# Where the spread reciprocals are copied: two exp steps behind their product, on VectorE in one unit, in an attention + MoE kernel

## The chip, the core and the metric

The kernel runs on one core of a Trainium2 chip. A core has TensorE (PE, the matmul array), VectorE (DVE), ScalarE (ACT), GpSimd (POOL) and SyncE (SP, here a queue for transfers). Each engine works through its own instructions in order and waits for the others by semaphores. The metric is the device time of one launch in microseconds; before the change the median of three runs is 494.64 us (494.27 to 496.47).

## The reference

```python
def _attn_ref(q, k, v):                 # (8, 12, 448, 64) each, f32
    scores = (1 / sqrt(64)) * q @ k.transpose(0, 1, 3, 2)
    m = max(scores, axis=-1, keepdims=True)
    e = exp(scores - m)
    attn = e / (sum(e, axis=-1, keepdims=True) + exp(-m) + 1e-09)
    return attn @ v

def _moe_ref(x, w_in, w_out):           # x (3584, 768), w_in (768, 2048), w_out (2048, 768)
    h = x @ w_in
    g = h * tanh(log1p(exp(h)))         # mish
    return g @ w_out

out = _moe_ref(attention, its heads side by side, w_in, w_out)
```

Eight batches of 12 heads of attention, with one added to the softmax's denominator, feed one MLP with a mish in the middle.

## The kernel before, in words

The work is cut in pairs of heads (6 pairs for a batch, 48 in all) and units of three pairs. The order of all instructions is written out by hand; no scheduler moves any. An "exp step" is one fourth of a pair: a step `s` of 0 to 3, numbered `idx = 4 * pair + s`. At a step, ACT computes the exps of one or two score tiles (`exps`, two instructions at steps 0 to 2, one at step 3). Then PE computes the scores of the step three further on, into one of three PSUM tiles `sc0` to `sc2`, and DVE finds their maxima (`negm`, in `scores`).

Everything else is put between the steps:

- `load_pair` (SP's queue), `cast_pair` (POOL): q, k and v come in and are cast to bf16.
- `transpose_pair` (PE), `evac_qk` (DVE or ACT): q and k are turned, and copied out of PSUM.
- `denominators` (DVE, POOL): the reciprocals `rden` of the row sums, and `hl`, the same as a sum of two bf16 numbers.
- `normalise`: `eT`, the turned exps, by a transposing DMA on SP's queue. For pairs 0 to 4 one of four quarters, and for pairs 5 to 7 (the dict `BY_PE`) all four, are turned by PE (`turn_on_pe`) and copied from PSUM by DVE, or by ACT where `TURN_BY_ACT` says so.
- `spread_rden` (pairs 0 to 11): 16 small matmuls spread a pair's reciprocals over the rows of a PSUM bank, from where ACT copies them to `rb` in SBUF.
- `av_pair`: eight matmuls multiply `eT` with v. For pairs 0 to 11, DVE multiplies the result by `rb` into `xT`; from pair 12 on (`LATE_DIV`) the exps were divided earlier, and DVE only copies.

There are two spare PSUM banks, `mo0` and `mo1`. `mo_take()` hands out one; it is given back where its copy out of PSUM is issued. Such copies are not issued at once: they go to the list `late`, which `flush_late()` issues behind the exps of the next step.

The stages: the head (pairs 0 to 5, the loop over `HEAD`), unit 2 (pairs 6 to 8), unit 3 (pairs 9 to 11), then units 4 to 15. Behind the steps of units 2 and later stand eight groups of matmuls with `w_in` and the mish on ACT (`mm1_mish`) for an earlier batch. From unit 4 on, matmuls with `w_out` (`mm2_part`) fill the gaps between the steps. The dicts `AV_AT` and `RDEN_AT` say at which step `n` of the unit a product or a spread stands in units 2 to 4: the outer key is the unit less 2, the inner one `n`, the value the pair.

In the head before the change, step 0 of pair p has `transpose_pair(p + 2)`, `denominators(p - 1)` and the turned quarter of p - 1; step 1 has the spread of p - 3, step 3 the product of p - 3.

Of the kernel before, what the change touches and what calls it, by code (L numbers as in the profile page):

```python
# [19 lines left out]
def kernel(  # L20
# [9 lines left out]
    nc = tc.nc  # L30

    B, H, S, D = q.shape
# [3 lines left out]
    NT = 4  # L36
# [63 lines left out]

    loaded, casted, qkT, att, xT, o_sbs, stats = {}, {}, {}, {}, {}, {}, {}
    av_with, av_read, rb = {}, {}, {}
    late = deque()

    def flush_late():
        while late:
# [2 lines left out]
    def mo_take():  # L109

        if not mo_free:
            flush_late()
        return mo_free.popleft()


    def load_pair(p):
# [205 lines left out]
            for i in range(n):  # L322
                att[p + i]["hl"] = hl[:, :, i, :]

    def spread_rden(p):

        own = mo_take()
        r = own[:, :]
        hl = att[p]["hl"]
        half = SP_ * NT - 3 * 128  # L330
        for at in range(4):
            for x in range(2):
                for h in range(2):
                    if at < 3:
                        rows, c, q0 = slice(0, 128), at + 4 * h, 128 * at + half * h
                    else:
                        rows, c, q0 = slice(half * h, half * h + half), 3, 3 * 128 * (1 - h)
                    n = rows.stop - rows.start
                    nc.tensor.matmul(  # L339
                        r[h * D : (h + 1) * D, q0 : q0 + n],  # L340
                        lhsT=hl[rows, x, c : c + 1].to_broadcast([n, D]),
                        rhs=ident[rows, rows],
                        start=(x == 0), stop=(x == 1),
                    )

        def evac():
            rb[p] = rb_pool.tile([128, S], FP32, tag="rb", name="rb")
            nc.scalar.copy(rb[p], r[:, 0:S])  # L348
            mo_free.append(own)

        late.append(evac)

    def normalise(p, dma=True):
        st = att[p]
# [30 lines left out]

        late.append(evac)

    def av_pair(p, bank=None, beside=None):
        b, hp = p // HP, p % HP
        eT = att[p]["eT"]  # L390
        v_bf = casted[p][2]
        if b not in xT:
            xT[b] = xT_pool.tile([128, DM_T, S], BF16, tag="xT", name="xT")
        av = mo_take() if bank is None else bank
        for j in range(NT):
            for h in range(2):
                if p >= DIAG_FROM:
                    by_h = eT[0:SP_, j, :].rearrange("c (i h r) -> c h i r", h=2, r=64)
                    e_h = by_h[:, h]
                else:  # L400
                    e_h = eT[0:SP_, j, h * S : (h + 1) * S]
                nc.tensor.matmul(  # L402
                    av[h * 64 : (h + 1) * 64, 0:S],
                    lhsT=v_bf[:, h, j * D : (j + 1) * D],
                    rhs=e_h,
                    start=(j == 0), stop=(j == NT - 1),
                )

        def evac():
            to = xT[b][:, hp, :]  # L410
            if p >= LATE_DIV:
                read = nc.vector.tensor_copy(out=to, in_=av[:, 0:S])  # L412
            else:
                read = nc.vector.tensor_tensor(
                    out=to, in0=av[:, 0:S], in1=rb.pop(p), op=ALU.mult
                )
            if beside is not None:
                av_read[beside] = read
            if bank is None:
                mo_free.append(av)  # L420

        late.append(evac)
        del att[p], casted[p], qkT[p]


# [94 lines left out]
    HEAD = HP  # L520

    BY_PE = {HEAD - 1: 1, HEAD: 0, HEAD + 1: STEPS}
    AV_AT = {0: {5: 3, 7: 4, 10: 5}, 1: {8: 6, 10: 7, 11: 8}}
    RDEN_AT = {0: {4: 3, 6: 4, 9: 5}, 1: {7: 6, 9: 7, 10: 8}, 2: {3: 10, 7: 11}}
    TURN_BY_ACT = {(HEAD - 1, 3), (HEAD, 3), (HEAD + 1, 2)}

    W_AT = ({1: 1, 5: 1, 9: 1}, {1: 1, 5: 1, 7: 1, 9: 1, 11: 1}, {1: 1, 3: 1, 5: 1, 7: 1})
    for p in range(UNIT_PAIRS):
# [13 lines left out]
    for p in range(HEAD):  # L542
        for s in range(STEPS):
            exps(p * STEPS + s)
            if s == 0 and p == 0:
                evac_qk(1, act=True)
            flush_late()
            if s == 2 and p < HEAD:
                evac_qk(p + 2, act=p % 2 == 0)
            scores_ahead(HEAD * STEPS + 3)  # L550
            if s == 0:
                transpose_pair(p + 2)
                if p:
                    denominators(p - 1)
                    turn_on_pe(p - 1, NT - 1)
            if s in (1, 3) and p == HEAD - 1:
                load_w(1)
            if s == 1 and p >= 3:
                spread_rden(p - 3)
            if s == 2:  # L560
                cast_pair(p + 3)
            if s == 3:
                if p >= 3:
                    av_pair(p - 3)
                if p + 5 < 10:
                    load_pair(p + 5)
                normalise(p, dma=p not in BY_PE)
    denominators(HEAD - 1)

    for u in range(UNITS_PER_B, N_UNITS + 2 * UNITS_PER_B):  # L570
        attn = u < N_UNITS
        filler = deque()
        for part in plan.get(u, []):
            filler.extend(mm2_part(*part))
        total, done, acc = sum(w for _, w in filler), 0, 0.0
        p0 = u * UNIT_PAIRS
        if attn and u >= first_mm2:
            av_with.update({p0 + i: p0 + i - UNIT_PAIRS for i in range(UNIT_PAIRS)})
        end = min((u + 1) * UNIT_PAIRS, N_PAIRS) * STEPS

        for n in range(steps):
            pi, s = divmod(n, STEPS)
            p, idx = p0 + pi, p0 * STEPS + n
            late_tp = u == UNITS_PER_B and n == STEPS
            if late_tp:
                transpose_pair(p0 + 2)
            exps(idx)
            if late_tp:
                evac_qk(p0 + 2)
            if u == UNITS_PER_B + 1 and n == 0:  # L590
                for j in range(2):
                    turn_on_pe(HEAD, j)
            flush_late()
            acc += weight[n]
            want = int(total * acc / sum(weight) + 1e-6)
            while done < want:
                fn, w = filler.popleft()
                fn()
                done += w
            scores_ahead(end)  # L600
            if n in LOAD_AT:
                load_pair(p0 + LOAD_AT.index(n) + LEAD)
                cast_pair(p0 + LOAD_AT.index(n) + LEAD - 1)
            spread = RDEN_AT.get(u - UNITS_PER_B, {})
            if n in spread:
                spread_rden(spread[n])
            early = AV_AT.get(u - UNITS_PER_B)
            if early is not None:
                if n in early:
                    av_pair(early[n])  # L610
                for pe, n0 in BY_PE.items():
                    first = 2 if pe == HEAD else 0
                    if pe // UNIT_PAIRS == u - 1 and n0 + first <= n < n0 + NT:
                        turn_on_pe(pe, n - n0, act=(pe, n - n0) in TURN_BY_ACT)
            elif s == (2 if pi else 0) and N_PAIRS <= p < N_PAIRS + UNIT_PAIRS:
                av_pair(p - UNIT_PAIRS)
            if u - UNITS_PER_B < len(W_AT):
                load_w(W_AT[u - UNITS_PER_B].get(n, 0))
        assert done == total

        moe = u < N_UNITS + UNITS_PER_B
        b, w = (u - UNITS_PER_B) // UNITS_PER_B, u % UNITS_PER_B
        nxt = p0 + UNIT_PAIRS
        todo = sorted(range(p0, nxt), key=lambda p: p in BY_PE)
        for f in range(FF_U):
            if moe:
                mm1_mish(b, w * FF_U + f)
            if u == UNITS_PER_B and f in (2, 6) or u == UNITS_PER_B + 1 and f == 1:
                load_w(1)
            if not attn:  # L630
                continue
            if f == 0:
                denominators(p0, UNIT_PAIRS)
                for p in todo if p0 < LATE_DIV else todo[:1]:
                    normalise(p, dma=p not in BY_PE)
            if f == 5 and u == UNITS_PER_B + 1:
                spread_rden(p0)
            if f == 4:
                scores_ahead(min(nxt * STEPS + 1, N_PAIRS * STEPS))
            if f in (1, 3, 5):  # L640
                transpose_pair(nxt + f // 2, bank=f // 2 % 2)
                evac_qk(nxt + f // 2)
            if f >= FF_U - 2:
                scores_ahead(min(nxt * STEPS + f - FF_U + 4, N_PAIRS * STEPS))
            if f in (3, FF_U - 1) and p0 >= LATE_DIV:
                p = todo[1 + f // (FF_U - 1)]
                normalise(p, dma=p not in BY_PE)
# [32 lines left out]
```

## Time and profile before

| | |
|---|---|
| median of three runs | 494.64 us |
| profiled execution, its own time | 492.1 us |
| its span, first to last instruction | 490.3 us |
| PE busy | 455.9 us (93%) |
| DVE busy | 356.3 us (73%) |
| ACT busy | 348.4 us (71%) |
| POOL busy | 103.3 us (21%) |
| mean granted clock of PE | 0.979 |

In the profile a row of the timeline has the start and the duration in us, the engine, the line of the kernel, the operation, out<-in, how many instructions were merged, and in brackets the idle time before them with who ended it. L296 are the exps, L283 the maxima, L339 the spread, L348 the copy `rb`, L376 a turned quarter and L380 its copy to `eT`, L402 the product with v, L414 its multiplication into `xT`, L431 and L437 the matmuls with `w_in` and the mish, L465 the copy of a finished output tile.

### The profile page before, as it was taken

To read this page: it belongs to the slowest core of one execution; us is meant where nothing else is said; L and a number is where in the kernel's file an instruction comes from. 1 tells how busy PE (TensorE), PEld (TensorE's weight loads), DVE (VectorE), ACT (ScalarE), POOL (GpSimd) and SP (SyncE) were. 2 spreads that over 40 slices of the span, in tenths; PEclk is the share of its full clock that TensorE was granted. 3 is DMA by queue.
4 is the path that set the end of the run, shared out by engine and by line. 5 is a ranking of instruction groups with operands and counts; after the bars stand their busy time and mean duration, and the time that the engine had idled before them with its cause. 6 is when DMAs were issued, how large, how long until landed. Compare 5 with 4: busy or idle time off the path is not lost.

```text
span 490.3 us, 9225 instructions
## 1 busy us (share of the span) xinstructions
PE 455.9 (93%) x3219; PEld 260.1 (53%) x3219; DVE 356.3 (73%) x706; ACT 348.4 (71%) x912; POOL 103.3 (21%) x184
## 2 busy tenths in 40 slices
PE   4676896898999999999999999999999999999996
PEld 2343553554555565555655555556555565556563
DVE  4887837657789898989989888889899988520011
ACT  5978778868788887978687978888797868402300
POOL 4533261423204040302213130404040200000000
PEclk9996698999999999999999999999999999999999
DMA  8999999999998969999899989997989786770122
GB/s 235 232 225 198 171 162 192 215 183 248 195 200 247 200 199 196 255 169 258 182 223 184 231 196 191 231 188 220 204 251 168 203 151 140 139 152 24 41 57 74
DMA packets 204975, 91.08 MB, mean 186 GB/s; under 512 B 161792, under 2 KB 201472, under 8 KB 204928
## 3 DMA queue, kind: packets, MB, share of 16 engines
q1 hardware_dynamic: 197440, 84.20, 80.5%
q0 software_dynamic: 7488, 6.29, 10.0%
q8 instruction: 25, 0.41, 0.4%
q14 instruction: 22, 0.18, 0.1%
HBM read 45.61 MB, written 11.01 MB: 115 GB/s over the span
## 4 chain that ended last, share of the span: by engine, by line
PE 68%; ACT 7%; DVE 5%; issue 1%; DVEq 0%
PE mo L431 25%; PE mo L478 23%; PE sc L262 7%; ACT en L296 6%; PE sc L402 6%; DVE negm L283 4%; PE sc L431 3%; PE sc L184 3%; PE mo L402 1%; DVE xT L412 1%; DVE o_sb L465 0%; PE mo L339 0%; ACT L296 0%; ACT rb L348 0%; ACT eT L380 0%
## 5 line engine op out<-in xcount | busy, mean ns | idle before, releaser
L296 ACT ACTIVATE en<-sc,negm 128x448 bf16<-128x448 f32 x336 | 208.6, 642 | 19.2 <-DVE negm L283 17.5
L283 DVE TENSOR_REDUCE negm<-sc 128x2 f32<-128x896 f32 x192 | 183.2, 971 | 45.2 <-PE sc L262 31.4
L478 PE MATMUL mo<-w_out_sb,gT 128*128 128x384 bf16 (+1 forms) x1024 | 166.7, 306 | 0.0
L431 PE MATMUL mo<-xT,w_in_sb 128*128 128x448 bf16 x672 | 141.8, 352 | 1.3 <-ACT rb L348 1.0
L478 PEld LDWEIGHTS <-gT 128*128 128x128 bf16 x1024 | 96.3, 98 | 55.4 <-issue 1.3
L437 ACT ACTIVATE gT<-mo 128x448 bf16<-128x448 f32 x112 | 59.5, 543 | 81.1 <-PE mo L431 81.0
L431 PEld LDWEIGHTS <-w_in_sb 128*128 128x128 bf16 x768 | 72.7, 98 | 64.3 <-issue 4.0
L164 POOL CAST q_bf<-q_f 112x512 bf16<-112x512 f32 x47 | 29.3, 623 | 239.7 <-DMA q_f<-in_q_dram 161.1
L357 DVE TENSOR_SCALAR en<-en,rden 128x448 bf16<-128x448 bf16 x252 | 73.4, 363 | 0.8
L296 ACT ACTIVATION_READ_ACCUMULATOR en<-sc,negm 128x1 f32 x336 | 71.9, 214 | 0.0
L262 PE MATMUL sc<-kT,qd 128*128 128x448 bf16 x252 | 71.6, 354 | 0.1
L465 DVE COPY o_sb<-mo 128x384 f32<-128x384 f32 (+1 forms) x64 | 32.1, 501 | 48.3 <-PE mo L478 48.1
L262 PEld LDWEIGHTS <-qd 128*128 128x128 bf16 x252 | 24.6, 98 | 29.2 <-issue 13.5
L402 PE MATMUL sc<-eT,v_bf 112*64 112x448 bf16 x288 | 34.1, 357 | 1.4 <-ACT en L296 0.9
L221 DVE TENSOR_SCALAR qd<-sc 64x448 bf16<-64x448 bf16 x72 | 27.8, 386 | 7.5 <-PE sc L184 6.7
L166 POOL CAST v_bf<-v_f 112x512 bf16<-112x512 f32 x48 | 29.8, 620 | 14.6 <-DMA v_f<-in_v_dram 13.7
L402 PEld LDWEIGHTS <-v_bf 112*64 112x64 bf16 x384 | 20.8, 111 | 21.6 <-issue 14.7
L165 POOL CAST k_bf<-k_f 112x512 bf16<-112x512 f32 x47 | 29.1, 619 | 5.6 <-DMA k_f<-in_k_dram 4.2
L268 PE MATMUL sc<-kT,qd 64*128 64x448 bf16 x36 | 16.0, 462 | 10.8 <-ACT en L296 10.2
L184 PEld LDWEIGHTS <-q_bf 112*128 112x128 bf16 x192 | 14.3, 103 | 14.6 <-DVE q_bf L164 4.2
L229 ACT COPY kT<-sc 128x448 bf16<-128x448 bf16 x39 | 20.8, 533 | 0.6 <-PE sc L184 0.6
L431 PE MATMUL sc<-xT,w_in_sb 128*128 128x448 bf16 x96 | 20.8, 353 | 0.0
(52 smaller groups left out, 283.0 us busy)
## 6 DMA issues: line engine op xcount, KB each, us to landing
q_f<-in_q_dram SPq DMA_DIRECT2D x48, 224.0 KB, 5.1
k_f<-in_k_dram SPq DMA_DIRECT2D x48, 224.0 KB, 5.3
v_f<-in_v_dram SPq DMA_DIRECT2D x48, 224.0 KB, 5.4
w_in_sb<-in_moe_w_in_dram POOLq DMA_DIRECT2D x12, 256.0 KB, 9.9
w_out_sb<-in_moe_w_out_dram POOLq DMA_DIRECT2D x8, 384.0 KB, 8.0
out_dram<-o_sb SPq DMA_DIRECT2D x7, 336.0 KB, 3.5
out_dram<-o_sb SPq DMA_DIRECT2D x8, 288.0 KB, 4.7
out_dram<-o_sb SPq DMA_DIRECT2D x8, 240.0 KB, 3.5
```

What stands on the lines that cost most here:

```text
L164: cast_q(out=q_bf, in_=q_f.rearrange(by_t, t=NT))
L165: cast_k(out=k_bf, in_=k_f.rearrange(by_t, t=NT))
L166: nc.gpsimd.tensor_copy(out=v_bf, in_=v_f)
L262: nc.tensor.matmul(sc[:, bk, 0:S], lhsT=qT[:, i].rearrange("d h r -> d (h r)"), rhs=kT, start=True, stop=True,)
L283: nc.vector.tensor_reduce(out=negm, in_=sc[:, 0 : len(cols), 0:S], axis=AX.X, op=ALU.max, negate=True)
L296: e = nc.scalar.activation(out=st["en"][:, :, c, 0:SP_], in_=sc[:, bk, 0:S].rearrange("q (j c) -> q j c", j=NT), func=AF.Exp, bias=st["neg ...
L357: nc.vector.tensor_scalar(out=en[:, :, i, 0:SP_], in0=en[:, :, i, 0:SP_], scalar1=st["rden"][:, i : i + 1], scalar2=None, op0=ALU.mult,)
L402: nc.tensor.matmul(av[h * 64 : (h + 1) * 64, 0:S], lhsT=v_bf[:, h, j * D : (j + 1) * D], rhs=e_h, start=(j == 0), stop=(j == NT - 1),)
L431: nc.tensor.matmul(h_ps[:, 0:S], lhsT=w_in_sb[:, dm, ff * 128 : (ff + 1) * 128], rhs=xT[b][:, dm, :], start=(dm == 0), stop=(dm == DM_T - 1),)
L437: nc.scalar.activation(out=gT[:, ff, b % 2 * S : b % 2 * S + S], in_=h_ps[:, 0:S], func=AF.Mish)
L465: nc.vector.tensor_copy(out=o_sb[:, cols], in_=st["o"][:, 0:n_cols])
L478: nc.tensor.matmul(st["o"][:, 0:n_cols], lhsT=gT[:, ff, i * 128 : (i + 1) * 128], rhs=w_out_sb[:, ff, cols], start=(ff == 0), stop=(ff == ...
```

## The change

The spread reciprocals are copied to `rb` later, and by another engine in some places.

- In the head, PE turns the quarter of pair p - 1 at step 1 and not at step 0, behind that step's scores. The spread moves from step 1 to step 2. Its copy is no longer issued at the next step: it is kept in `spread_copy` until the pair's product is issued at step 3, and goes out behind the exps of step 0 of the next pair. The product's own copy (`xT`) is kept one step more, in `held`, and goes out behind the exps of step 1. The last copy of the head goes out behind the loop, before the exps of unit 2.
- In unit 2 the spreads of pairs 3 and 4 move one step back (n = 5, 7), their products too (n = 6, 8); pair 5 stays (n = 9, 10). The copies, still on ACT, go out two steps behind the spread, next to the product's.
- In units 3 and 4 the copies of pairs 6, 7, 8, 10 and 11 go to DVE, one step behind their spread as before. The copy of pair 9 stays on ACT.
- All quarters turned by PE in unit 3 are copied by DVE; two of them were ACT's. In unit 2 one stays with ACT.

Nothing is added to or taken from the computation.

```diff
-    late = deque()
+    late, held = deque(), deque()
...
+    spread_copy = {}
...
-    def spread_rden(p):
+    def spread_rden(p, copy=None):
...
         def evac():
             rb[p] = rb_pool.tile([128, S], FP32, tag="rb", name="rb")
-            nc.scalar.copy(rb[p], r[:, 0:S])
+            (copy or nc.scalar.copy)(rb[p], r[:, 0:S])
             mo_free.append(own)
 
-        late.append(evac)
+        if copy is None:
+            spread_copy[p] = evac
+        else:
+            late.append(evac)
...
-    def av_pair(p, bank=None, beside=None):
+    def av_pair(p, bank=None, beside=None, hold=False):
...
-        late.append(evac)
+        if p in spread_copy:
+            late.append(spread_copy.pop(p))
+        (held if hold else late).append(evac)
         del att[p], casted[p], qkT[p]
...
-    AV_AT = {0: {5: 3, 7: 4, 10: 5}, 1: {8: 6, 10: 7, 11: 8}}
-    RDEN_AT = {0: {4: 3, 6: 4, 9: 5}, 1: {7: 6, 9: 7, 10: 8}, 2: {3: 10, 7: 11}}
-    TURN_BY_ACT = {(HEAD - 1, 3), (HEAD, 3), (HEAD + 1, 2)}
+    AV_AT = {0: {6: 3, 8: 4, 10: 5}, 1: {8: 6, 10: 7, 11: 8}}
+    RDEN_AT = {0: {5: 3, 7: 4, 9: 5}, 1: {7: 6, 9: 7, 10: 8}, 2: {3: 10, 7: 11}}
+    TURN_BY_ACT = {(HEAD - 1, 3)}
...
             flush_late()
-            if s == 2 and p < HEAD:
+            if s == 1:
+                late.extend(held)
+                held.clear()
+                flush_late()
+            if s == 2:
                 evac_qk(p + 2, act=p % 2 == 0)
             scores_ahead(HEAD * STEPS + 3)
             if s == 0:
                 transpose_pair(p + 2)
                 if p:
                     denominators(p - 1)
-                    turn_on_pe(p - 1, NT - 1)
+            if s == 1 and p:
+                turn_on_pe(p - 1, NT - 1)
             if s in (1, 3) and p == HEAD - 1:
                 load_w(1)
-            if s == 1 and p >= 3:
-                spread_rden(p - 3)
             if s == 2:
+                if p >= 3:
+                    spread_rden(p - 3)
                 cast_pair(p + 3)
             if s == 3:
                 if p >= 3:
-                    av_pair(p - 3)
+                    av_pair(p - 3, hold=True)
...
     denominators(HEAD - 1)
+    flush_late()
+    late.extend(held)
...
-                spread_rden(spread[n])
+                spread_rden(spread[n], copy=None if u == UNITS_PER_B else nc.vector.tensor_copy)
...
             if f == 5 and u == UNITS_PER_B + 1:
-                spread_rden(p0)
+                spread_rden(p0, copy=nc.scalar.copy)
```

## The prediction, made before the changed kernel ran

> **What bounds the kernel now.** I read the profiled page first, then the busy time by stage, then the waits of ScalarE (ACT) and VectorE (DVE) in the early stages, then the timeline row by row from 8 to 125 us.
>
> ```profile
> PE 455.9 (93%) x3219; PEld 260.1 (53%) x3219; DVE 356.3 (73%) x706; ACT 348.4 (71%) x912; POOL 103.3 (21%) x184
> PEclk9996698999999999999999999999999999999999
> ```
> ```profile
> core 0: us, PE busy (x) PEld busy (x) DVE busy (x) ACT busy (x) POOL busy (x), PEclk, DMA share, GB/s
> 24.93:45.63 20.70, 14.77 (x133) 8.69 (x133) 16.68 (x28) 15.74 (x52) 7.45 (x18) 0.84 1.08 226
> 45.63:64.14 18.51, 15.26 (x136) 8.97 (x136) 13.53 (x22) 15.09 (x47) 6.34 (x13) 0.72 1.24 175
> 77.28:95.56 18.28, 12.25 (x132) 8.18 (x131) 12.25 (x17) 17.16 (x49) 6.39 (x10) 0.91 1.18 225
> 109.39:125.00 15.61, 13.46 (x114) 7.42 (x113) 10.42 (x15) 13.49 (x43) 6.82 (x11) 1.00 1.12 246
> 125.00:475.00 350.00, 349.12 (x2359) 198.39 (x2357) 269.81 (x568) 251.92 (x646) 53.89 (x88) 1.00 0.84 183
> ```
>
> The rows are: pairs 3 to 5 of the head, unit 2 (pairs 6 to 8) up to its first mm1 matmul, unit 3 (pairs 9 to 11) up to the same point, unit 4, and the rest. From 125 us on TensorE (PE) is busy 349.12 of 350 us, so the change, which adds no matmul, can't shorten that stretch; whatever it moves earlier before 125 us arrives at the end unchanged. The early stages are different: no engine fills them. In the first two rows ACT idles 4.96 and 3.42 us, and DVE 4.02 and 4.98 us. What holds ACT there:
>
> ```profile
> ACT rb L348 <- PE mo L339: 7.9, 5, 2.4
> ACT en L296 <- DVE negm L283: 3.6, 4, 2.4
> ```
> ```profile
> 28.58 0.62 DVE L380 COPY eT<-mo 112x896 bf16<-112x896 bf16 x1 [0.60 <-PE mo L376]
> 29.26 1.09 PE L339 MATMUL mo<-ident,hl 128*64 128x128 bf16 x16 [0.23 <-DVE eT L380]
> 30.40 0.53 ACT L348 COPY rb<-mo 128x448 f32<-128x448 f32 x1 [1.63 <-PE mo L339]
> 55.27 0.53 ACT L348 COPY rb<-mo 128x448 f32<-128x448 f32 x1 [2.36 <-PE mo L339]
> ```
>
> Of 8 to 64.2 us, ACT spends 7.9 us in five waits of the rb copy. The rows show why: the turned quarter of eT holds one of two mo banks; DVE copies it (28.58), then PE spreads the reciprocals into that bank (29.26), then ACT copies them (30.40). ACT's exps stand behind that copy in order, and their maxima were already there.
>
> **The change, part by part.** No DMA changes place, and the orders on POOL and SyncE (SP) are the same; the two mo banks swap names for the rest of the run, which costs nothing. The matmuls are the same in number and only change place before 65 us.
>
> *Pairs 1 and 2 of the head.* PE does the next scores before the turned quarter, and DVE the next maximum before its copy.
>
> ```profile
> 19.34 0.63 ACT L296 ACTIVATE en<-sc,negm 128x448 bf16<-128x448 f32 x1 [0.80 <-DVE negm L283]
> 24.93 0.67 ACT L296 ACTIVATE en<-sc,negm 128x448 bf16<-128x448 f32 x1
> 31.55 0.63 ACT L296 ACTIVATE en<-sc,negm 128x448 bf16<-128x448 f32 x1
> 38.25 0.65 ACT L296 ACTIVATE en<-sc,negm 128x448 bf16<-128x448 f32 x1
> 45.63 0.63 ACT L296 ACTIVATE en<-sc,negm 128x448 bf16<-128x448 f32 x1
> ```
>
> These are the first exps of pairs 2 to 6. The 0.80 us wait at 19.34 was a maximum behind such a copy. It goes, but the copy (0.62) and the two copies of q and k then stand before the next maximum, so most comes back one exp step later. I count 0.2 us (bounds 0 and 0.8).
>
> *Pairs 3 to 5.* They take 6.62, 6.70 and 7.38 us. Now the reciprocals are spread at step 2, copied by ACT after the exps of the next pair's step 0, and the product's DVE copy (xT) follows at step 1. The five waits lose their cause: two exp steps lie between product and copy. What is late next is DVE: its busy time is 16.68 / 3 = 5.56 us for a pair, against 15.74 / 3 = 5.25 on ACT. Pair 2, which has no rb and no xT, took 24.93 - 19.34 = 5.59; with the rb copy (0.53 in the rows above, a little less where the next instruction overlaps it) on ACT and xT's 0.5 or so on DVE beside it, a pair is 6.0 to 6.1. I take 6.05: 20.70 - 3 x 6.05 = 2.55, rounded 2.6. Bounds: 5.56 gives 4.0; 6.5, if half of the removed wait comes back as waits for maxima, gives 1.2.
>
> *Unit 2.* ACT's idle time here is 3.42 us.
>
> ```profile
> 56.14 0.91 ACT L380 COPY eT<-mo 112x896 bf16<-112x896 bf16 x1 [0.34 <-PE mo L376]
> 63.94 0.69 ACT L296 ACTIVATE en<-sc,negm 128x448 bf16<-128x448 f32 x1
> 64.14 2.43 PE L431 MATMUL mo<-xT,w_in_sb 128*128 128x448 bf16 x12 [1.00 <-ACT rb L348]
> ```
>
> The eT copy that ACT keeps (56.14) still waits: its quarter needs a mo bank that the transposes of pair 8 and their two DVE copies must free first. That is a chain of an eT copy (0.62), the transposes, two copies and the turned quarter, some 2.8 us by my count, against one step of two exps, 1.2. I leave 1.6 us of the idle time there, so 1.8 us go. The last rb copy moves from before the last exp to behind it: 0.4 us off the exps. But the first mm1 matmul takes the bank which that copy frees. Today it starts 0.2 us after the last exp's start; then it is the exp (0.6) and the copy (0.53) later, about 1.2. So 1.0 us is lost at this seam, and nothing hides it, as PE has nothing else in its queue. The last rb of the head also waits ahead of unit 2's first exp; DVE's queue is the longer there, so I put nothing on it (cost without that cover: 1.2, a wait like the others). Sum 1.8 + 0.4 - 1.0 = 1.2 (0 to 2.4).
>
> *Unit 3.* Two turned quarters and three rb copies go from ACT to DVE.
>
> ```profile
> L380 DVE COPY eT<-mo 112x896 bf16<-112x896 bf16 x6 | 3.6, 616 | 0.2 <-PE mo L376 0.2
> L380 ACT COPY eT<-mo 112x896 bf16<-112x896 bf16 x2 | 1.8, 905 | 1.1 <-PE mo L376 0.7 <-ACT en L296 0.4
> L348 ACT COPY rb<-mo 128x448 f32<-128x448 f32 x3 | 1.7, 568 | 0.0
> 80.37 2.32 DVE L283 TENSOR_REDUCE negm<-sc 128x2 f32<-128x896 f32 x2 [0.60 <-PE sc L271]
> 87.29 0.61 DVE L380 COPY eT<-mo 112x896 bf16<-112x896 bf16 x1
> 87.82 2.08 DVE L283 TENSOR_REDUCE negm<-sc 128x2 f32<-128x896 f32 x2
> 90.64 0.95 PE L402 MATMUL mo<-eT,v_bf 112*64 112x448 bf16 x8
> 95.56 2.44 PE L431 MATMUL mo<-xT,w_in_sb 128*128 128x448 bf16 x12
> ```
> ```profile
> L465 DVE COPY o_sb<-mo x3: 348/548/548, 113.2 to 125.0; 128x384 f32<-128x384 f32 x2, 128x192 f32<-128x192 f32 x1
> ```
>
> ACT loses 1.8 + 1.7 us of work and 1.1 us of waiting and is no longer the bound. DVE gets 2 x 0.616 and 3 x about 0.57 more (an f32 PSUM copy of 384 columns takes 0.548, the product of 448 columns 0.61): 12.25 + 2.95 = 15.2 of 18.28. It is then busy without a gap from 80.37: six maxima of two banks at 1.04 (2.08 / 2), two of one bank at 0.55, six eT copies at 0.53 (87.29 to 87.82) and one rb at 0.53 are 11.1 us, so the last maximum is there at 91.5. Behind it is a chain through the banks: rb of pair 6, av (0.95), xT (0.6), the last spread (0.7), its rb (0.55), the last av (0.95), each with about 0.1 for the hand-over, 4.3 us from 90.5: mm1 starts at 94.8 instead of 95.56. I count 0.7 (bounds: -1.0, if the chain starts at 92.2 because the clock is at half, and +2.0).
>
> The Trainium skill, VectorE: DVE Perf Modes, Specifications, places ScalarE closer to PSUM and VectorE closer to SBUF, which speaks against moving PSUM reads to DVE. Here the rows disagree: the same 112x896 tile takes ACT 905 ns and DVE 616. By the page the two moved tiles would cost DVE 0.905 or more, 0.6 us more in all, and unit 3 would gain 0.1.
>
> *Unit 4.* Two more rb copies go to DVE, each ahead of a one-bank maximum that waits for PE anyway:
>
> ```profile
> 117.52 0.62 DVE L283 TENSOR_REDUCE negm<-sc 128x1 f32<-128x448 f32 x1 [0.78 <-PE sc L262]
> 123.90 0.62 DVE L283 TENSOR_REDUCE negm<-sc 128x1 f32<-128x448 f32 x1 [1.64 <-PE sc L262]
> ```
>
> Both gaps are longer than a copy, so it costs nothing (1.1 if they weren't there). ACT loses its wait there, but the next exps wait for maxima: no gain.
>
> **Sum:** 0.2 + 2.6 + 1.2 + 0.7 + 0 = 4.7 us. The profiled execution took 492.1 us (span 490.3): 487.4. It is 2.5 us below the median of the timed runs, 494.64; taking the gain off that median gives **489.9 us**.
>
> **The rivals.**
>
> *Everything comes back.* PE's clock is at half in parts of these stages:
>
> ```profile
> 50.00:52.00 2.00, 2.00 (x15) 1.34 (x14) 2.00 (x5) 1.81 (x6) 0.61 (x1) 0.50 1.20 129
> ```
>
> If PE, with fewer gaps, is granted the full rate throughout, all 7.9 us of rb waits go, less 1.0 at the seam and with 0.7 in unit 3: 7.6 us, **487.0**. For it: the mean clock of these stages is 0.84 and 0.72, so there is time to win back. Against: DVE's 5.56 a pair caps the head's part at 4.0, and the row above shows PE busy 2.00 of 2.00 at clock 0.50, so density alone didn't lift it. The Trainium skill, TensorE: Matmul & The Clock Gate, What's actually happening, says that about 3.4 us of sustained work open the full rate; by that rule this rival would be the likeliest, and this trace shows the rule only in part. Chance 0.12.
>
> *DVE paces.* The waits for rb turn into waits for maxima: a pair takes 6.5, unit 2 and unit 3 give nothing: 1.2 us, **493.4**. For it: ACT already waits 3.6 us for maxima, and xT in unit 2 waits for rb with maxima behind it. Chance 0.17.
>
> *The banks run short.* Spread and product now hold both mo banks until steps 0 and 1 of the next pair; the turned quarter needs the bank which xT frees, and the next scores stand behind it on PE, their maximum behind that on DVE.
>
> ```profile
> 27.60 0.95 PE L376 MATMUL mo<-ident,en 128*112 128x128 bf16 x7
> L414 DVE TENSOR_TENSOR xT<-mo,rb 128x448 bf16<-128x448 f32 x6 | 3.7, 613 | 2.7 <-ACT rb L348 1.8 <-PE mo L402 0.9
> ```
>
> If that chain is not covered by exps in hand, each of six pairs (3 to 8) waits 0.61 + 0.95 = 1.56: 9.4 us in place of 7.9, and with the 1.0 at the seam and nothing from unit 3 it is 2.5 slower: **497.1**. It decides once the maxima for two steps ahead aren't ready, which a half clock would bring; by my order of events one step and a half are. Chance 0.11.
>
> *SP paces.* By the timeline SP's queue works without a gap from the first to the last of these:
>
> ```profile
> 14.07 8.43 SPq L365 DMA_TRANSPOSE eT<-en  x1
> 42.71 8.43 SPq L365 DMA_TRANSPOSE eT<-en  x1
> ```
>
> That is four loads and transposes in 28.64 us, 7.2 a pair, and the change doesn't touch it. If products or casts come to wait for them, the head keeps its pace: **494.6**. Against: the transpose that starts at 14.07 ends at 22.5, and the product that reads it comes only behind the spread at 29.26, so a lead of some 7 us is there to be eaten first. Chance 0.05.
>
> **How the numbers follow.** The forecast has 0.55; its own range, 488.0 to 491.8, comes from the parts' bounds taken half way. About 0.5% (2.5 us) is what a measurement of this kernel can tell from no change. Faster by more: 0.54 of the forecast, 0.12, and 0.03 of DVE pacing, 0.69. Slower by more: 0.11 for the banks and 0.01 of the seam, 0.12. The rest, 0.19, is within. The range goes from the full return, 487.0, to 494.0, which takes in DVE pacing and leaves out the banks, SP and a little at the low end.
>
> **What would show it.** Right: no wait of ACT's rb for PE over 0.5 us before 64 us; first exps of pairs 3 to 6 some 6 us apart; the first mm1 matmul near 60 us, waiting for rb about 1 us after the last exp's start; in unit 3 ACT waiting for maxima and DVE without gaps; then the same PE-filled stretch, 4 to 5 us earlier. Wrong: ACT's waits for negm grown by as much as those for rb shrank, PE waiting for xT ahead of the turned quarter, or a lower granted clock from 25 to 60 us.

## The result, and the profile after

The forecast was 489.9 us, with a range from 487.0 to 494.0. The changed kernel takes 491.52 us (median of 20 runs) against 493.48 (20 runs of the kernel before beside them): ratio 0.995 [0.9926, 0.9974], or some 2.5 us less (1.3 to 3.7). It was timed twice more beside other kernels: 491.82 against 493.30, ratio 0.9978 [0.9954, 1.0002], and 491.48 against 493.73, ratio 0.9979 [0.9952, 1.0006]. By the ratios the gain is 2.5, 1.1 and 1.0 us, and the last two intervals reach up to no change: the direction is that of the forecast, the size a fifth to a half of its 4.7. The profiled execution took 488.69 us with a span of 486.9; the one of before took 492.1 and 490.3.

The page of the changed kernel, first busy times and then the granted clock of PE in 40 slices:

```profile
PE 453.3 (93%) x3219; PEld 258.4 (53%) x3219; DVE 359.4 (74%) x713; ACT 345.4 (71%) x905; POOL 103.4 (21%) x184
PEclk9999798999999999999999999999999999999999
```

Three us of work went from ACT to DVE, as the edit says. The fourth and fifth slice of the clock (37 to 61 us), 6 and 6 before, are 9 and 7. Its busy time by stage, columns as before (length, busy time and count of PE, PEld, DVE, ACT, POOL, then clock, DMA share, GB/s):

```profile
25.20:43.71 18.51, 14.36 (x139) 8.14 (x140) 16.17 (x28) 16.03 (x52) 7.19 (x18) 1.00 1.11 226
43.71:61.30 17.59, 13.46 (x134) 8.05 (x131) 13.58 (x22) 15.60 (x49) 8.20 (x15) 0.81 1.16 248
74.43:91.57 17.14, 11.98 (x132) 8.01 (x132) 14.63 (x22) 14.96 (x44) 6.02 (x10) 0.90 1.00 187
105.39:120.54 15.15, 12.45 (x110) 7.03 (x109) 10.68 (x15) 12.71 (x40) 7.38 (x12) 1.00 1.14 251
125.00:475.00 350.00, 348.83 (x2357) 198.58 (x2356) 267.45 (x557) 248.06 (x637) 53.22 (x87) 1.00 0.84 182
```

The first three rows run between the same events as those of before: pairs 3 to 5 take 18.51 (20.70 before), unit 2 up to its first mm1 matmul 17.59 (18.51), unit 3 up to its first mm1 matmul 17.14 (18.28). The fourth ends at the first mm1 matmul of unit 4, which the row of before does not. The last row is the same stretch full of PE work. What ACT waited for from 8 to 62 us, the three largest (total, times, longest):

```profile
ACT en L298 <- DVE negm L285: 3.4, 3, 2.4
ACT rb L350 <- PE mo L341: 2.3, 3, 1.6
ACT eT L385 <- PE mo L381: 1.6, 1, 1.6
```

The waits of the rb copy shrank from 7.9 us to 2.3 (0.35, 1.63 and 0.29), and those for maxima did not grow (3.6, now 3.4). One long wait is left, the head's last rb copy ahead of unit 2's first exp, and the timelines of DVE, PE and ACT show what it stands behind:

```profile
41.83 0.61 DVE L385 COPY eT<-mo 112x896 bf16<-112x896 bf16 x1
42.49 0.70 PE L341 MATMUL mo<-ident,hl 128*64 128x128 bf16 x16 [0.69 <-DVE eT L385]
43.28 0.53 ACT L350 COPY rb<-mo 128x448 f32<-128x448 f32 x1 [1.63 <-PE mo L341]
43.71 0.64 ACT L298 ACTIVATE en<-sc,negm 128x448 bf16<-128x448 f32 x1
```

That is the old chain (quarter's copy, spread, rb) once more, because here the copy goes out ahead of the exps and not two steps behind its spread.

### The profile page after: what moved, and what is told of

The parts are those of the page before. It is cut to its first block, busy times and chain, and to the rows that moved or that the text cites. A ratio compares the mean times of both kernels' runs of the same rounds, so it can differ in the third digit from the quotient of the medians.

```text
span 486.9 us, 9223 instructions
## 1 busy us (share of the span) xinstructions
PE 453.3 (93%) x3219; PEld 258.4 (53%) x3219; DVE 359.4 (74%) x713; ACT 345.4 (71%) x905; POOL 103.4 (21%) x184
## 4 chain that ended last, share of the span: by engine, by line
PE 75%; ACT 11%; DVE 8%; DMA 2%; issue 2%; SPq 1%; POOL 0%; DVEq 0%; ACTq 0%
PE mo L438 26%; PE mo L485 24%; ACT en L298 9%; PE sc L264 7%; DVE negm L285 6%; PE sc L407 5%; PE sc L438 4%; PE sc L186 3%; PE mo L407 2%; DMA k_f<-in_k_dram 1%; PE mo L341 1%; PE sc L270 1%; DMA v_f<-in_v_dram 1%; SPq L125 1%; DVE eT L385 1%
```

## The experiments

Two theories stood against each other, as the expectations name them: W, the gain is what ACT no longer waits for spread copies; C, it is the clock that PE was granted in this or that execution. The intervals below all compare with runs of the kernel before on the same chip.

**The changed kernel, and its parts alone (beside the same runs of before).** First, the kernel unchanged:

> The changed kernel as it is, once more, as the measure for the others and for a second trace. Over 20 runs it took 0.995 of the kernel before; its first trace had TensorE's clock at 1.00 in pairs 3 to 5 of the head where the trace before had 0.84. Theory W (the waits of the rb copy were the cost): the first mm1 matmul near 61.3 us and unit 3's near 91.6 again, whatever the clock, and a ratio of 0.994 to 0.997. Rival C (the clock was the cost): where the mean clock from 25 to 43 us is below 0.9, the head's gain is mostly gone, and the first mm1 matmul comes at 63 us or later.

Second, the new order of the head and of unit 2 alone:

```diff
-    TURN_BY_ACT = {(HEAD - 1, 3)}
+    TURN_BY_ACT = {(HEAD - 1, 3), (HEAD, 3), (HEAD + 1, 2)}
...
-    spread_rden(spread[n], copy=None if u == UNITS_PER_B else nc.vector.tensor_copy)
+    spread_rden(spread[n], copy=None if u == UNITS_PER_B else nc.scalar.copy)
```

> The head's and unit 2's new order alone; units 3 and 4 copy on ScalarE as before the change. Theory W: the first mm1 matmul near 61.3 us, as in the changed kernel; unit 3 then lasts 18.3 us from its first exp to its mm1, as before, not 17.1; in all 1.1 us above the changed kernel, 1.3 us or so below the kernel before (ratio 0.997). Rival D (what DVE was given is the gain): no gain is left, ratio 1.000 or above.

Third, into the kernel before, only the copies of pairs 6, 7, 8, 10 and 11 and the turned quarters on DVE:

```diff
-    TURN_BY_ACT = {(HEAD - 1, 3), (HEAD, 3), (HEAD + 1, 2)}
+    TURN_BY_ACT = {(HEAD - 1, 3)}
...
-    spread_rden(spread[n])
+    spread_rden(spread[n], copy=None if u == UNITS_PER_B else nc.vector.tensor_copy)
```

> The copies of units 3 and 4 on DVE alone; head and unit 2 in the order before the change. Theory W: the first mm1 matmul at 64 us, as before; unit 3 lasts 17.1 us and not 18.3: 1.1 us below the kernel before, ratio 0.998. Rival D: the whole gain, ratio 0.995. If DVE's copies cost more than ScalarE's release is worth, it is over 1.000.

Fourth, the changed kernel with the copy one step behind its spread, as it was before:

```diff
-        if copy is None:
-            spread_copy[p] = evac
-        else:
-            late.append(evac)
+        late.append(evac)
```

> The changed kernel, but in the head and unit 2 the rb copy goes out one exp step behind its spread instead of two (the spread stays at its new place, the product's copy too). Theory W: ScalarE waits for the spread again, 1 to 1.8 us in each of pairs 3 to 5 and less in unit 2, 4 to 6 us of such waits in place of 2.3; the first mm1 matmul 2 us or more later than in the changed kernel, near 63.5, ratio 0.999. Rival Q (what helps is that scores go ahead of the turned quarter and the spread, the copy's place is nothing): no change against the changed kernel, mm1 near 61.3.

Measured: 491.82 (0.9978), 492.48 (0.998 [0.9957, 1.0004]), 492.30 (0.9985 [0.9958, 1.0013]) and 492.29 (0.9984 [0.9951, 1.0018]). Four kernels within 0.7 us of each other cannot be told apart by time, so neither half is sized here and the second step of delay is not shown to matter. In the fourth's trace ACT waited for rb three times in pairs 3 to 5, 1.4 to 1.8 us each and 4.9 in all, as W's mark has it; yet these pairs took 20.68 us with scores of 510 ns, and 20.48 with 492 in the changed kernel's third trace (told below). So what the second step saves there stays open. (This execution was a long one for another reason, PE waiting 7.3 us for w_out to land in unit 4.)

By the place of the first mm1 matmul the traces are divided. The changed kernel's second trace has it at 65.17 us, where W had 61.3 whatever the clock, and C 63 or later at a clock below 0.9; it was 0.91 from 25 to 43 us and 0.88 over pairs 3 to 5. (A wait for a DMA has a part in this, see the rivals below.) In the early order alone it comes at 60.92, as W had it, and in DVE's copies alone at 61.49, where W had 64. The rows say more. The old order of the head, in the third kernel, pairs 3 to 5:

```profile
25.23:44.01 18.78, 12.38 (x133) 7.66 (x133) 15.97 (x28) 15.78 (x53) 6.42 (x17) 1.00 1.01 230
```

This is the order that took 20.70 us in the profile before. What differs is how fast PE ran, and the durations of the score matmuls tell it better than the clock column. They take about 0.36 us in a stretch where PE is fast and about 0.55 where it is slow; the groups of the scores from pair 3 to pair 5 (busy time, mean ns of one) mix both. The kernel before, its second trace (the run is told below), and DVE's copies alone, all in the old order:

```profile
L268 PE MATMUL sc<-kT,qd 64*128 64x448 bf16 x9 | 4.0, 450 | 3.6 <-ACT en L296 3.6
```
```profile
L268 PE MATMUL sc<-kT,qd 64*128 64x448 bf16 x9 | 4.1, 459 | 3.5 <-ACT en L296 3.5
```
```profile
L268 PE MATMUL sc<-kT,qd 64*128 64x448 bf16 x9 | 3.6, 397 | 3.7 <-ACT en L296 3.7
```

The stages are 20.70, 21.14 and 18.78 us long. In the new order, the changed kernel, the early order alone, and the changed kernel in its third trace (told below too):

```profile
L270 PE MATMUL sc<-kT,qd 64*128 64x448 bf16 x10 | 4.3, 434 | 0.7 <-ACT en L298 0.7
```
```profile
L270 PE MATMUL sc<-kT,qd 64*128 64x448 bf16 x10 | 4.5, 454 | 0.8 <-ACT en L298 0.8
```
```profile
L270 PE MATMUL sc<-kT,qd 64*128 64x448 bf16 x10 | 4.9, 492 | 0.8 <-ACT en L298 0.8
```

Here they are 18.51, 18.95 and 20.48 us long. So at the same PE speed (450 and 459 against 454) the new order is 1.75 to 2.2 us shorter, and one execution with a slow PE loses as much again. Both theories have hold of something; which decides the time needed a kernel in which PE's speed does not wander.

**Both kernels with more PE work in the early stages.** The score matmuls of pairs 0 to 11 are issued twice, the second of them writing the same again; the question is whether the order still makes a difference where PE has more to do.

```diff
-            nc.tensor.matmul(sc[:, 0, 0:S], ...)
-            nc.tensor.matmul(sc[:, 1, 0:S], ...)
+            for _ in range(2):
+                nc.tensor.matmul(sc[:, 0, 0:S], ...)
+                nc.tensor.matmul(sc[:, 1, 0:S], ...)
```

Kernel before, scores twice:

> The kernel before, with the score matmuls of pairs 0 to 11 issued twice into the same bank (the second overwrites the first with the same numbers), so that TensorE has fewer idle stretches and its granted clock stays up. In the five traces so far the clock from pair 3 to pair 8 differs from run to run (0.68 to 1.00). Theory C (most of the early gain in the first pair of traces was the clock): at a clock near 1.00 the old order takes some 18.8 us from the first exp of pair 3 to that of pair 6, and 49 to 51 us from pair 3 to pair 9, although its ScalarE still waits some 4 us for the spread. Theory W (the waits for the spread cost what they last): 20 us or more, and 52 us, whatever the clock.

Changed kernel, scores twice:

> The same in the changed kernel: score matmuls of pairs 0 to 11 twice. Theory C: at equal clock it is within 1 us of the other from pair 3 to pair 9 (some 49 us). Theory W: 3 us or more less than the other. In units 3 and 4 both theories have it 1 us ahead, by what went from ScalarE to DVE.

The kernel before, for a second trace:

> The kernel before, once more, for a second trace. Theory C: if its clock from 25 to 64 us is above the 0.84 and 0.73 of the first trace, the stretch from pair 3 to pair 9 is shorter than its 52.35 us, by up to 2; if below, longer. Theory W: 52 us either way.

Measured: 493.90 (1.0024 [1.0003, 1.0044]) and 489.86 (0.994 [0.9922, 0.9958]). With doubled scores the two orders are 0.84% apart, some 4 us, with intervals far from each other: this speaks against C, which has no place for a difference tied to the order. But not all of the 4 us need be waits. In its trace the kernel before with doubled scores had 7.0 us of waits of rb and took 20.44 us for pairs 3 to 5 with scores of 421 ns; the same order with scores of 358 ns, told below, takes 19.32. From pair 3 to pair 9 it is 51.48 us against 48.31 in the new order, W's 3 us.

The second trace of the kernel before took 51.62 us from pair 3 to pair 9. Its clock was 0.65 over pairs 3 to 5 and 0.90 in unit 2, below the first trace's in the one and above it in the other, so this decides nothing. It had 7.5 us of waits of rb (7.9 in the first).

What the doubling does to PE is seen in the score rows of the changed kernel. Without it, on PE's timeline:

```profile
28.01 0.55 PE L270 MATMUL sc<-kT,qd 64*128 64x448 bf16 x1
33.50 0.58 PE L278 MATMUL sc<-kT,qd 64*64 64x448 bf16 x1
34.56 0.36 PE L270 MATMUL sc<-kT,qd 64*128 64x448 bf16 x1
```

With it:

```profile
21.46 0.57 PE L280 MATMUL sc<-kT,qd 64*64 64x448 bf16 x1
23.26 0.35 PE L271 MATMUL sc<-kT,qd 64*128 64x448 bf16 x1 [0.66 <-ACT en L300]
```

PE turns fast at 23 us and not at 34, and in this trace its scores stay at 0.34 to 0.37 us to the end of unit 2. The Trainium skill, TensorE: Matmul & The Clock Gate, What's actually happening, has PE at half rate by default and at full rate behind a window of some 3.4 us in which it was busy. The two traces above agree with it; the kernel before with doubled scores does not plainly, as its scores stay at 0.53 to 0.58 us from 15.85 to 30.80 us. The clock column does not show this: it reads 1.00 for the plain kernel from 25.20 to 43.71 us, the 0.55 rows included.

**The halves, with doubled scores.** The edits are those of the second and third kernel above, each with the doubled scores.

> The score matmuls of pairs 0 to 11 are issued twice, as in the two kernels of 493.9 and 489.86 us; of the change only the new order of the head and of unit 2 is in, all copies and turned quarters of unit 3 stay on ACT. Theory W (waits of ACT for the spread in the early stage): it keeps the early part of the 4 us and loses unit 3's 1 to 1.5, so about 491.2 us, ACT's waits for spread copies up to 62 us near 2, and first exps of pairs 3 and 9 about 48.5 to 49 us apart. Theory C (the granted clock of each execution, not the order, makes the difference): no nearer to the one than to the other, and pairs 3 and 9 at 51 or more wherever the clock of the stage is under 0.8.

> Scores twice as before; of the change only the copies and turned tiles on DVE are in, with the old order of the head and of unit 2. Theory W: unit 3's 1 to 1.5 us and unit 2's quarter of about 1, so about 492 us, ACT's waits for spread copies up to 62 us still 4 to 6, pairs 9 to 12 about 1.2 shorter than the 33.5 of the old division. If the whole 4 us stem from unit 3 (a theory U): 490 us, and the kernel with the early order alone 494.

> The changed kernel itself once more, timed beside the three above. Theory W: 0.995 of the kernel before, or 490.9 us where that takes 493.4. If doubling the scores is a gain by itself through a higher clock (theory H): over 1 us above 489.86, and the profile's stage from pair 3 to pair 6 under a clock of 0.9.

Measured: the early order alone 491.78 (0.996 [0.9944, 0.9976]), DVE's copies alone 492.86 (0.9991 [0.9974, 1.0007]), the changed kernel without doubling 491.48 (0.9979). In per cent of the kernel before, the early order brings 1.0024 - 0.996 = 0.64% (3.2 us), DVE's copies 1.0024 - 0.9991 = 0.33% (1.6 us); both together 0.84% (4.1 us). Added up they give 4.8, about the whole, and with the early order's 3.2 theory U (all from unit 3) falls. DVE's 1.6 is not shown by time alone: its interval touches that of the kernel before with doubled scores, [1.0003, 1.0044]. ACT's waits for rb fit W's marks: 1.6 us in the early order alone, which took 48.33 us from pair 3 to pair 9, and 5.9 in DVE's copies alone. That the doubling makes the changed kernel itself faster (H) is likely: 0.994 [0.9922, 0.9958] against 0.995, 0.9978 and 0.9979, with intervals that overlap. H's clock of 0.9 in the plain kernel did not come; the column reads 1.00 where the scores, at 492 ns, were slowest.

Where the early part lies can now be read at one speed of PE, since in both kernels shown next the scores of pairs 3 to 8 are nearly all fast (in the kernel before with doubled scores they are not). Stages from the traces: pairs 3 and 4, pair 5, pairs 6 to 8 (unit 2 with the mish behind it), pairs 9 to 11 (the same of unit 3), always from first exp to first exp. Old order with DVE's copies, scores twice:

```profile
25.91:38.29 12.38, 8.25 (x102) 4.52 (x102) 11.13 (x18) 10.77 (x37) 4.12 (x11) 1.00 0.99 228
38.29:45.23 6.94, 6.00 (x55) 3.08 (x55) 5.17 (x10) 4.96 (x18) 2.98 (x7) 0.75 1.21 209
45.23:76.27 31.04, 26.39 (x254) 13.87 (x254) 19.65 (x31) 23.83 (x63) 12.57 (x23) 1.00 1.24 169
76.27:107.88 31.61, 27.48 (x255) 15.88 (x255) 22.97 (x40) 22.66 (x58) 10.02 (x17) 0.95 1.20 175
```

The whole change, scores twice:

```profile
25.87:36.44 10.57, 7.84 (x86) 4.12 (x86) 9.75 (x17) 10.27 (x36) 3.90 (x11) 1.00 1.08 220
36.44:43.49 7.05, 5.80 (x77) 3.11 (x78) 6.38 (x12) 5.41 (x20) 3.29 (x8) 1.00 0.96 210
43.49:74.18 30.69, 25.74 (x250) 13.74 (x251) 19.71 (x31) 23.74 (x62) 12.55 (x23) 1.00 1.23 194
74.18:106.62 32.44, 28.75 (x255) 16.31 (x255) 23.21 (x40) 22.66 (x57) 10.02 (x17) 0.89 1.22 212
```

The groups of their scores over pairs 3 to 5, in the same order:

```profile
L269 PE MATMUL sc<-kT,qd 64*128 64x448 bf16 x18 | 5.0, 358 | 3.0 <-ACT en L298 3.0
```
```profile
L271 PE MATMUL sc<-kT,qd 64*128 64x448 bf16 x20 | 5.4, 352 | 1.2 <-ACT en L300 1.1
```

Pairs 3 and 4 gain 1.81 us; pair 5 is 0.11 longer, unit 2 with its mish 0.35 shorter. The last rows are both of the new unit 3. The same stage with the old unit 3, in the kernel before and in the early order alone, scores twice:

```profile
78.05:111.54 33.49, 29.05 (x255) 16.17 (x255) 20.52 (x35) 25.09 (x62) 10.08 (x17) 0.90 1.05 172
```
```profile
74.36:107.63 33.27, 27.73 (x255) 15.88 (x255) 20.52 (x35) 25.09 (x62) 10.08 (x17) 0.95 1.14 197
```

The four stages pair off by the speed of their scores: 33.49 and 32.44 with means of 453 and 458 ns, 33.27 and 31.61 with 418 and 402. So the move to DVE takes 1.05 to 1.66 us off.

**The wait that was left.** On the changed kernel the head's last rb copy goes out behind the first exps of unit 2, and the last quarter that ACT copied goes to DVE:

```diff
     denominators(HEAD - 1)
-    flush_late()
     late.extend(held)
...
-    TURN_BY_ACT = {(HEAD - 1, 3)}
+    TURN_BY_ACT = set()
```

> The changed kernel with two of its waits moved away: the last rb copy of the head goes out behind the first exps of unit 2 instead of before them, and the quarter that ScalarE still copied in unit 2 goes to DVE. In the trace of the changed kernel ScalarE waited 1.6 us before each and copied 0.8 us. Theory W: both waits go, 2 us below the changed kernel at the first mm1 matmul, ratio 0.992 to 0.994. Theory C: the maxima are late anyway (DVE and TensorE at their clock), under 0.7 us, ratio 0.995 to 0.998.

The same with doubled scores:

> Scores twice, the changed kernel's whole order, and besides the head's last spread copy behind the first exps of unit 2 and the last quarter turned for ACT given to DVE. Theory W: the 1.6 us for which ACT stood ahead of unit 2 goes, so 488.5 us against 489.86. Rival (the copy only stands elsewhere, ACT waits for maxima instead): 489.9 within 1 us.

Measured: 491.33 (0.9968 [0.9944, 0.9992]) without doubling, no difference from the changed kernel that shows, and in C's range; with doubling 489.25 (0.9911 [0.9888, 0.9933]), the fastest kernel here, 0.6 us by the medians and 0.29% by the ratios below the 489.86, with overlapping intervals, between the two forecasts. In the traces with doubled scores the place is plain; pair 5 took 7.05, and now:

```profile
36.26:41.53 5.27, 4.52 (x55) 2.30 (x55) 4.61 (x9) 4.99 (x18) 1.36 (x4) 1.00 1.32 200
41.53:72.27 30.74, 26.88 (x272) 14.36 (x271) 20.99 (x35) 23.93 (x60) 14.61 (x26) 1.00 1.19 206
```

1.78 us go from pair 5 and 0.05 come back in unit 2. ACT then has no wait for a spread left at all up to 60 us:

```profile
ACT en L300 <- DVE negm L287: 6.4, 11, 2.7
```

Its waits for maxima rose from 4.8 to 6.4, so of W and its rival both have a part: the 1.64 us of rb and 1.4 of eT go, 1.6 return as waits for maxima, and the span is 1.6 us shorter (486.5 against 488.1). Without doubled scores pair 5 is as short (5.30), but unit 2 with its mish took 33.55 us in that execution against 30.72 in the changed kernel's first trace, and the gain does not show. In that trace PE's product of pair 4 waited for `eT`, which a DMA turns:

```profile
58.71 1.40 PE L407 MATMUL mo<-eT,v_bf 112*64 112x448 bf16 x8 [2.10 <-DMA eT<-en]
```

## Why the prediction was right in mechanism and too high in size

*The chain.* Right in the main: with two exp steps between spread and copy the five waits of 7.9 us are down to three of 2.3, and only the head's last is over the 0.5 us that was named. In unit 2 the eT copy waits 1.58 us where 1.6 was left for it. The first mm1 matmul starts 1.3 us after the last exp does, where 1.2 was forecast, but that number is luck in part: it was to wait for rb with nothing else in PE's queue, and in fact PE was at the last product until 61.04 and waited for rb only 0.26 us. On ACT and PE of the changed kernel:

```profile
52.38 0.91 ACT L385 COPY eT<-mo 112x896 bf16<-112x896 bf16 x1 [1.58 <-PE mo L381]
59.99 0.64 ACT L298 ACTIVATE en<-sc,negm 128x448 bf16<-128x448 f32 x1
60.70 0.54 ACT L350 COPY rb<-mo 128x448 f32<-128x448 f32 x1
60.09 0.95 PE L407 MATMUL mo<-eT,v_bf 112*64 112x448 bf16 x8 [0.27 <-DVE xT L419]
61.30 0.92 PE L438 MATMUL mo<-xT,w_in_sb 128*128 128x448 bf16 x4 [0.26 <-ACT rb L350]
```

*Pairs 1 and 2, forecast 0.2.* Right, and in the way forecast. From the first exp of pair 1 to that of pair 3 the two traces of the kernel before take 10.97 and 10.96 us, the three of the changed kernel 10.74 to 10.76. The wait of 0.80 us at 19.34 is gone, and one exp step later most of it is back:

```profile
21.20 0.63 ACT L298 ACTIVATE en<-sc,negm 128x448 bf16<-128x448 f32 x1 [0.79 <-DVE negm L285]
```

The first exp of pair 3 is at 25.20 us all the same, and at 24.93 before, because pair 1 began at 14.46 in this execution and at 13.96 before. No edit stands ahead of pair 1; in the changed kernel's other traces it began at 13.89 and 13.96.

*Pairs 3 to 5, forecast 2.6.* Somewhat too high: at equal PE speed 1.75 to 2.2 without and 1.7 (19.32 against 17.62) with doubled scores. The forecast pace of 6.05 a pair was too slow for pairs 3 and 4, 5.3 each with a fast PE, and too quick for pair 5, 7.05, for the reason next. In the first trace, too, the pairs are not some 6 us each but 4.60, 6.85 and 7.06.

*The last rb of the head, priced at nothing.* This step failed: "DVE's queue is the longer there" does not hold; ACT waited 1.63, 2.65 and 2.31 us in the three traces, and 1.64 with doubled scores. The cost given without that cover, 1.2, was the better value. With wait and copy moved away, pair 5 takes 5.27.

*Unit 2, forecast 1.2.* Right for the PE speed at which it was read, too high for a fast one. Its row of before was 18.51 with scores of 462 ns; the changed kernel's first and third trace, with 444 and 448, took 17.59 and 17.22 up to the first mm1 matmul, 0.9 to 1.3 less. But the kernel before took 17.35 in its second trace, with 380 ns, and the changed kernel 20.33 in its own second, for a reason told under the rivals. With doubled scores, 350 ns in both orders, it is 45.23 to 62.77 against 43.49 to 60.67, or 0.36:

```profile
62.77 2.05 PE L433 MATMUL mo<-xT,w_in_sb 128*128 128x448 bf16 x10 [0.81 <-ACT rb L350]
```
```profile
60.67 1.11 PE L440 MATMUL mo<-xT,w_in_sb 128*128 128x448 bf16 x5 [0.77 <-ACT rb L352]
```

ACT's idle time of 3.42 us in the row of before was thus partly a slow PE's, which no order of the copies gives back.

*Unit 3, forecast 0.7.* Right in kind: ACT stops being the bound, DVE runs on and the chain of the banks follows. It brought 1.14 us in the first pair of traces, whose scores took 382 and 387 ns, and 1.05 to 1.66 with doubled scores, within the bounds; the changed kernel's other two traces took 17.45 and 17.48. DVE has no gap from 77.52 to 89.75 us. The end of that stretch and the chain behind it:

```profile
85.94 1.08 DVE L285 TENSOR_REDUCE negm<-sc 128x2 f32<-128x896 f32 x1
86.94 0.62 DVE L350 COPY rb<-mo 128x448 f32<-128x448 f32 x1
87.47 0.62 DVE L385 COPY eT<-mo 112x896 bf16<-112x896 bf16 x1
90.01 0.62 DVE L350 COPY rb<-mo 128x448 f32<-128x448 f32 x1 [0.27 <-PE mo L341]
91.68 0.62 DVE L419 TENSOR_TENSOR xT<-mo,rb 128x448 bf16<-128x448 f32 x1 [0.16 <-PE mo L407]
```

Each moved copy cost DVE 0.53 from start to start, a little under what was counted: its busy time in the stage rose by 2.4 us (12.25 to 14.63), not by 2.95. No quarter cost 0.905. The Trainium skill, VectorE: DVE Perf Modes, Specifications, places ScalarE closer to PSUM; this trace still speaks against a choice by that, with 0.61 on DVE and 0.91 on ACT for the same tile.

*Unit 4, forecast 0.* It cost a little: from its first exp to its first mm1 matmul 15.15 us, against 14.90 before (109.39 to 124.29). Ahead of the last spread PE waited 1.40 us for DVE's copy of an output tile, where it had waited 1.10, and ahead of a product 0.68 us for an exp, where it had waited 0.30. The other traces bear the size out: 14.91 in the second trace of before and in the early order alone, 15.14 or 15.15 in the changed kernel's other two and in DVE's copies alone. From there to the end the changed kernel takes 366.4 us and the one before 366.0; no row read here shows why.

*The rivals.* DVE did not pace: the waits for maxima stayed. Of the banks' chain the first link is there; the turned quarters of pairs 3 to 5 waited 1.5 us for xT in all:

```profile
L381 PE MATMUL mo<-ident,en 128*112 128x128 bf16 x21 | 2.1, 252 | 1.5 <-DVE xT L419 1.5
```

As I read the rows, it reached ACT only at the head's last rb copy, where no exps stand between, so the price of 1.56 fell due about once and not six times. "Everything comes back" rests on PE at full rate, and the doubled kernels came nearest to it; they show why it is not 7.6: the head's last wait and the eT copy's stay.

*SP's queue* was given 0.05, for a lead of some 7 us that was read at the product of pair 0. The head did not keep its pace, but by the product of pair 4, in unit 2, that lead is used up. In the kernel before, the transpose for it is issued at 42.71 us and lands 15.5 us later, at 58.2; the product starts at 59.56. In the changed kernel ACT gets there earlier and the transpose does not: it is issued at 43.52, 42.53 and 44.61 us in the three traces and lands after 11.6, 18.4 and 14.7. The first trace does not wait for it; the second and the third do:

```profile
61.01 1.71 PE L407 MATMUL mo<-eT,v_bf 112*64 112x448 bf16 x8 [1.41 <-DMA eT<-en]
59.33 0.95 PE L407 MATMUL mo<-eT,v_bf 112*64 112x448 bf16 x8 [0.58 <-DMA eT<-en]
```

The second is the trace in which unit 2 took 20.33 us. In the five traces with doubled scores the same transpose lands 8.2 to 12.6 us after its issue, and this product never waits for it. Why it lands sooner there is not shown; so part of what those kernels gain may be this and not the speed of PE.

*The sum.* At the PE speed of the trace from which it was made, the measured terms are 0.2, 1.75 to 2.2, 0.9 to 1.3, 1.1 and a loss of 0.25, or 3.7 to 4.6 where the sum had 4.7; the two first profiles are 3.4 us apart. The doubled kernels are 4.1 us apart. The plain kernels are only 1.0 to 2.5 us apart, and this is the step that failed: the sum took for granted that PE runs as fast in the changed kernel as in the one trace of before, and that the transposes land in time, as they did there. In its second and third trace pairs 3 to 5 took 20.20 and 20.48 us, with scores of 473 and 492 ns, so that the gain of that stage was all but gone, and in unit 2 both waited for a transpose. Why PE is slow for longer in some executions is not known. In the three plain traces of the old order the scores of pairs 3 to 5 took 397 to 459 ns, in the six of the new one 434 to 510; whether the new order brings that about, so few traces cannot tell, and it stays open.

## What to carry to other kernels

Before the length of a stage is used in a sum, look at what one matmul of a fixed shape takes there: lengths can be subtracted only at the same speed of PE, and a stage with gaps on PE can run at two speeds in two executions of one program. When a copy is moved away from its producer, follow every instance to the seams of its loop; the one that is issued early at the loop's end keeps the whole wait. A lead over a transfer has to be read at every product that needs it, not only at the first. Where two orders differ by less than this wandering, add the same spare matmuls to both and compare them there, stage by stage where the length of one matmul is the same: the old order kept slow stretches even so.

## What the runs showed of the hardware that was not expected

More matmuls made the changed kernel no slower and probably faster: doubled scores in 12 pairs took the changed kernel from 0.995, 0.9978 and 0.9979 of the time before to 0.994, and with the last wait gone to 0.9911, while the kernel before went to 1.0024. PE, with its scores at 0.53 to 0.58 us for nearly all of the time from 9 to some 30 to 40 us in the plain traces, kept to 0.34 to 0.37 from 23 us to the end of unit 2 in the changed kernel with doubled scores; in the kernel before with them it was slow from 15.85 to 30.80 us and again from 41.9 to 44.4. The column of the granted clock missed most of this: it read 1.00 over stages in which the mean score took 492, 434 or 352 ns.
